# Second layer's first product by Strassen's scheme, and another series for small h

## The chip, the cores and the metric

The kernel runs on one core of one Trainium2 chip. The metric is the device time of one execution in microseconds (us), as the median of several runs. TensorE is called PE here and its weight loads PEld, VectorE DVE, ScalarE ACT, and SP is the engine that issues all the DMAs. fc counts the 16 blocks of 128 hidden columns of a layer.

## The reference, cut to what matters

```python
p_packed = sm_attn(p, k, v)             # 8 batches, 8 heads, 576 tokens, 64 wide, 32 packed
out = sm_attn(q, p_packed, p_packed)    # softmax attention twice
x = out as (4608 tokens, 512)
# first layer
h = x @ moe_w_in                        # 512 -> 2048
x = (h * tanh(softplus(h))) @ moe_w_out # 2048 -> 512
# second layer
h = x @ moe2_w_in                       # 512 -> 2048
return (h - tanh(h)) @ moe2_w_out       # 2048 -> 512
```

All is fp32. The difference h - tanh(h) loses digits for small h; there the kernel takes a series in h*h instead, chosen element by element.

## The kernel before

A product in fp32 accuracy is done as three passes of fp32r matmuls (PASSES): each operand is a high half and a low half (high times high, high times low, low times high). For each fp32 tile, ACT copies the high half and DVE subtracts to get the low half.

The kernel has two stages. The first (attention and first layer) works through 8 batches of two halves of 288 tokens: attention makes x, `layer1` takes h of two fc at a time (L580), applies Mish on ACT (L584), splits (L586, L587) and accumulates the second product (L598). Its outputs y go to DRAM (`y_d`). During this stage the weights of the second layer, which arrive as 64-bit words, are also decoded (`dec_unit`), split (`dec_split`) and written to DRAM as `w2i_d` and `w2o_d`.

The second stage works through 9 blocks of 512 tokens, and in each through 16 fc (`layer2`, 144 in all). Of one fc, PE makes h[128, 512] in one PSUM bank from four K blocks of 128 with three passes each: 12 matmuls of 512 columns (L665). ACT and DVE turn h into g: Square of h (L671), two more Squares with a pointer bias (L672, L673), Tanh (L674), three products on DVE for the series (L675, L677, L679), the difference (L681), the comparison (L683), the choice (L685), the high half (L686) and the low half (L687). PE then makes the second product: for four output blocks oc three matmuls of 512 columns each (L696), accumulated over all 16 fc in four banks `acc`. Four more banks (`bk`) hold the h's in flight. All weights of the second layer lie in SBUF in this stage: w2i in the tiles `m`, `x` and `xw`, w2o in `wo`. `load_y` brings a block's y, four K blocks, and splits each (L647, L648).

The order of the work is set by a planner, `Plan`. Each operation has an engine, a duration, a key (its due time) and the buffers that it takes and gives back; the planner steps through its own time and gives each free engine the ready operation with the smallest key. Buffers of a kind that has a queue are handed out in the order of keys. The instructions are emitted in that order, so each engine's order is fixed at build time, and semaphores keep the dependencies.

## Time and profile before

| | |
|---|---|
| median of three runs | 1557.94 us (1557.05 to 1559.39) |
| the profiled execution | 1557.33 us, its span 1555.6 us |
| mean granted clock of PE | 0.992 |
| PE busy | 1517.1 us, 98% |
| DVE busy | 1018.8 us, 65% |
| ACT busy | 899.0 us, 58% |

The span is the time from the first to the last instruction in the trace; an execution's time is a little longer. Busy times of PE are modelled ends of pipelined matmuls, so neighbours overlap, and the rate is read from starts, not from durations. An idle time in brackets stands with what ended it.

### The profile page before, as it was taken

Reading aid. Unit: us, or ns where it says so; the run is one execution under the profiler, and the core shown is the slowest. Engines: PE = TensorE matmul, PEld = TensorE weight load, DVE = VectorE, ACT = ScalarE, POOL = GpSimd, SP = SyncE. Lnnn points to the kernel's source line nnn. Section 1 sums busy time; section 2 is a strip of 40 time slices with the busy share of each in tenths; the row PEclk is TensorE's granted clock in tenths of the full one; section 3 lists DMA queues with packets and bytes.
Section 4 is the critical chain, followed back from the end, with each engine's and each line's share of the span. In section 5 each row is a group of like instructions: output and inputs, shape, how many; then the busy total and the mean of one; then the engine's idle time right before and its main releaser. Section 6 shows DMA issues by size and latency. Waiting matters only on the chain.

```text
span 1555.6 us, 24595 instructions
## 1 busy us (share of the span) xinstructions
PE 1517.1 (98%) x9816; PEld 1305.9 (84%) x9816; DVE 1018.8 (65%) x1699; ACT 899.0 (58%) x1640; POOL 0.2 (0%) x4
## 2 busy tenths in 40 slices
PE   4699999999999999999999999999999999999998
PEld 1498889999998989899988888888888888888887
DVE  6956665555634333332198888888888888888886
ACT  5866766656554545554365556565655555565654
POOL 0000000000000000000000000000000000000000
PEclk9699999999999999999999999999999999999999
DMA  8677664755625232244801001010100001010000
GB/s 296 204 269 268 224 225 171 232 191 179 215 84 163 71 118 88 82 140 143 292 1 28 28 11 44 1 55 1 54 2 27 28 15 41 1 55 1 28 1 27
DMA packets 78275, 159.48 MB, mean 103 GB/s; under 512 B 7888, under 2 KB 25424, under 8 KB 78160
## 3 DMA queue, kind: packets, MB, share of 16 engines
q1 hardware_dynamic: 78160, 157.91, 30.5%
q8 instruction: 77, 1.26, 0.3%
q14 instruction: 38, 0.31, 0.1%
HBM read 118.03 MB, written 39.85 MB: 101 GB/s over the span
## 4 chain that ended last, share of the span: by engine, by line
PE 93%; DVE 3%; ACT 2%; DMA 1%; issue 0%; SPq 0%; DVEq 0%; ACTq 0%
PE acc L598 26%; PE acc L696 25%; PE bk L665 25%; PE bk L580 13%; PE bk L548 2%; PE bk L418 1%; DMA st<-in_w1o 1%; PE bk L466 1%; PE bk L492 0%; PE bk L445 0%; DMA x<-in_k 0%; ACT st L311 0%; DMA st<-in_w1i 0%; DVE m L556 0%; DVE rr L318 0%
## 5 line engine op out<-in xcount | busy, mean ns | idle before, releaser
L696 PE MATMUL acc<-g,wo 128*128 128x512 f32 x1728 | 482.0, 389 | 0.6 <-ACT g L686 0.3
L598 PE MATMUL acc<-g,wo 128*128 128x288 f32 x3072 | 440.3, 297 | 0.0
L598 PEld LDWEIGHTS acc<-g,wo 128*128 128x128 f32 x3072 | 417.6, 189 | 17.1 <-issue 15.8
L696 PEld LDWEIGHTS acc<-g,wo 128*128 128x128 f32 x1728 | 324.3, 188 | 68.6 <-ACT g L686 0.8
L671 ACT ACTIVATE e<-bk 128x512 f32<-128x512 f32 x144 | 86.1, 598 | 316.2 <-PE bk L665 315.3
L587 DVE TENSOR_TENSOR g<-e,g 128x576 fp32r<-128x576 f32 x128 | 96.9, 757 | 229.8 <-ACT g L586 228.5
L580 PEld LDWEIGHTS bk<-a,m 128*128 128x128 f32 x1536 | 212.9, 190 | 31.1 <-issue 10.1
L580 PE MATMUL bk<-a,m 128*128 128x288 f32 x1536 | 232.0, 300 | 5.4 <-ACT a L518 4.3
L584 ACT ACTIVATE e<-bk 128x288 f32<-128x288 f32 x256 | 103.6, 412 | 154.9 <-PE bk L580 150.5
L681 DVE TENSOR_TENSOR tt<-bk,tt 128x512 f32<-128x512 f32 x144 | 99.5, 691 | 122.5 <-ACT tt L674 122.5
L665 PE MATMUL bk<-a,m 128*128 128x512 f32 x432 | 121.3, 390 | 0.8 <-DVE s L679 0.8
L665 PE MATMUL bk<-yh,m 128*128 128x512 f32 x432 | 121.2, 389 | 0.0
L685 DVE COPY_PREDICATED s<-mk,tt 128x512 f32<-128x512 uint32 x144 | 108.7, 755 | 4.4
L677 DVE SCALAR_TENSOR_TENSOR s<-s,s 128x512 f32<-128x512 f32 x144 | 99.5, 691 | 13.6 <-DVE s L675 0.9
L672 ACT ACTIVATE s<-e,c_qb 128x512 f32<-128x512 f32 x144 | 104.2, 723 | 1.1 <-DVE g L687 1.1
L673 ACT ACTIVATE s<-e,c_qd 128x512 f32<-128x512 f32 x144 | 103.7, 720 | 0.3 <-DVE s L677 0.2
L679 DVE SCALAR_TENSOR_TENSOR s<-s,bk 128x512 f32<-128x512 f32 x144 | 98.9, 687 | 4.5
L687 DVE TENSOR_TENSOR g<-s,g 128x512 fp32r<-128x512 f32 x144 | 98.3, 683 | 3.8 <-ACT g L686 3.8
L675 DVE SCALAR_TENSOR_TENSOR s<-s,e 128x512 f32<-128x512 f32 x144 | 98.7, 686 | 0.2 <-ACT s L672 0.2
L686 ACT ACTIVATE g<-s 128x512 fp32r<-128x512 f32 x144 | 90.9, 631 | 9.1 <-DVE s L685 9.1
L665 PEld LDWEIGHTS bk<-a,m 128*128 128x128 f32 x432 | 80.8, 188 | 18.1 <-DVE s L679 1.6
L665 PEld LDWEIGHTS bk<-yh,m 128*128 128x128 f32 x432 | 81.0, 188 | 16.7
...
## 6 DMA issues: line engine op xcount, KB each, us to landing
...
```

Of the source, the lines that this page charges most:

```text
L580: T.matmul(h.tile[:, :HALF], r(m.tile[:, fc % 4, kc, wl, :]), r(x.tile[:, kc, al, :]), start=(i == 0), stop=(i == 5))
L584: fr.append(op("ACT", a_cost(HALF, True), lambda c=c, h=h: A.activation(e.tile[:, c, :], h.tile[:, :HALF], AF.Mish), kf + 1, [g1] + fr, [e ...
L598: T.matmul(ac.tile[:, :HALF], r(wo[fc].tile[:, wl, oc * 128:(oc + 1) * 128]), r(gt.tile[:, gl, c, :]), start=(fc == 0 and i == 0), stop=(f ...
L665: T.matmul(h.tile, r(wv[:, wl, :]), r(yh[blk, kc].tile[:, yl, :]), start=(kc == 0 and i == 0), stop=(kc == 3 and i == 2))
L672: p1 = op("ACT", a_cost(TB, False, True), lambda: A.activation(s1.tile, zz.tile, AF.Square, bias=c_qb), k0 + 1.1, [sq], [s1])
L673: p2 = op("ACT", a_cost(TB, False, True), lambda: A.activation(s2.tile, zz.tile, AF.Square, bias=c_qd), k0 + 1.2, [sq], [s2])
L675: q = op("DVE", v_cost(TB), lambda: V.scalar_tensor_tensor(out=s1.tile, in0=s1.tile, scalar=Q_C, in1=zz.tile, op0=ALU.add, op1=ALU.mult), ...
L677: q = op("DVE", v_cost(TB), lambda: V.scalar_tensor_tensor(out=s1.tile, in0=s2.tile, scalar=Q_E, in1=s1.tile, op0=ALU.add, op1=ALU.mult), ...
L679: q = op("DVE", v_cost(TB), lambda: V.scalar_tensor_tensor(out=s1.tile, in0=s1.tile, scalar=Q_A, in1=h.tile, op0=ALU.mult, op1=ALU.mult), ...
L681: d = op("DVE", v_cost(TB), lambda: V.tensor_tensor(out=tt.tile, in0=h.tile, in1=tt.tile, op=ALU.subtract), k0 + 1.6, [th], give=[h])
L685: q = op("DVE", v_cost(TB), lambda: V.copy_predicated(s1.tile, mk.tile, tt.tile), k0 + 1.8, [q, d, k], give=[mk, tt])
L696: T.matmul(ac.tile, r(w2c[fc].tile[:, wl, oc * 128:(oc + 1) * 128]), r(gt.tile[:, gl, :]), start=(fc == 0 and i == 0), stop=(fc == NFC - 1 ...
```

## The change

Two fc that lie 8 apart (p and p+8, `NPAIR` = 8 pairs) and two halves of 256 tokens of a block make a 2 by 2 block product, with the two halves of K (256 each) summed over. Before it was 8 products of 128 x 256 x 256, now it is 7, in Winograd's form of Strassen's scheme. With A the weights (first index the fc half, second the K half) and B the tokens (first index the K half, second the token half):

```
S1 = A10 + A11   S2 = S1 - A00   S3 = A00 - A10   S4 = A01 - S2
T1 = B01 - B00   T2 = B11 - T1   T3 = B11 - B01   T4 = T2 - B10
P1 = A00 B00   P2 = A01 B10   P5 = S1 T1   P6 = S2 T2   P3 = S4 B11   P7 = S3 T3   P4 = -A11 T4
h00 = P1 + P2   h01 = P1 + P6 + P5 + P3   h11 = P1 + P6 + P7 + P5   h10 = P1 + P6 + P7 + P4
```

Every product is 2 K blocks x 3 passes = 6 matmuls of 256 columns (`product`, L761). P1, P6, P7 and P4 accumulate in one bank, and ACT copies the bank out in between (`c1`, `cy`, and `c21` at the end); P5 and P3 share a second bank (`c5` after P5), P2 has a third. DVE adds bank and copy into the tile of h in SBUF (`c11`, `c12`, `c22`, L775). So h is read from SBUF afterwards, not from PSUM.

The sums S and their splits are made in the first stage (`dec_pair`): from two decoded tiles seven tiles of high and low halves, each written to `w2i_d` (256 KB). In the second stage a pair's weights are loaded anew for every block (1,024 and 768 KB into `m`, four buffers), and are not kept. `load_y` makes the sums T and seven splits for each block, with two loads of 512 KB.

The series for small h is now (sigmoid(Q_L z + Q_B) + Q_E) * tanh(Q_T z) * Q_A * h with z = h*h: two activations as before, both of the table set `sigmoid_and_others`, which also holds Square, Tanh and Copy, so that the stage still has one table load; and two products on DVE for three. The comparison is written over z (the tile `e`). The border between series and difference moves from z = 0.3 to 0.2. The planner's period of a pair, TP, is 10.5 (5.25 an fc before), and due times are given in fifteenths of it.

```diff
-NB = NBLK * NFC
+NB = NBLK * NFC // 2
 SCALE = 1.0 / math.sqrt(D)
-ZSEL = 0.3
+ZSEL = 0.2
 LOW = 0.937 * 2.0 ** -29
-Q_B, Q_C, Q_D, Q_E = 0.6608551084240504, 6.240764296453553, -2.29454690082585, 2.410061604415441
-Q_A = 0.006504088563070549
+
+Q_T, Q_L, Q_B, Q_A, Q_E = 0.4706837657198442, -1.185665545740827, -5.582744233256905, 63.98041875880057, 0.007320721938160889
...
-    for nm, n in (("tt", 2), ("yf", 2), ("s1", 2), ("s2", 2), ("mk", 2), ("yh", 3), ("o", 1)):
+    for nm, n in (("yh", 7), ("tt", 2), ("pc", 6)):
...
-    w2i_d = dr.tile([16, 128, 2, 2, 2, 128], F32, name="w2i_d")
+    w2i_d = dr.tile([NPAIR, 128, 7, 2, 2, 128], F32, name="w2i_d")
...
+    def dec_pair(p, key):
+
+
+        u = Buf(K["so"], [128, 2, 512])
+        f = []
+        for i in range(2):
+            f.append(dec_unit(w2i[p + 8 * i], key + 0.5 * w2_step * i,
+                              lambda i=i: u.tile[:, i, :].rearrange("p (k f) -> p k f", k=4), [u] if i == 0 else [],
+                              False, True, f))
+
+        def q(i, j):
+            return u.tile[:, i, 256 * j:256 * j + 256]
+
+
+        steps = ((0, None, (0, 0), 1), (1, None, (0, 1), 1), (6, None, (1, 1), -1),
+                 (5, "s3", None, 1), (2, ((1, 0), ALU.add, (1, 1)), (1, 0), 1),
+                 (3, ((0, 0), ALU.subtract, (1, 0)), (0, 0), 1), (4, ((0, 1), ALU.subtract, (0, 0)), (0, 1), 1))
+        last, ends = f, []
...
+            h = op("ACT", a_cost(256), lambda ov=ov, sv=sv, sign=sign: A.activation(
+                r(ov(0)), sv(), AF.Copy, scale=float(sign)), k, last, take)
+            l = op("DVE", v_cost(256), lambda ov=ov, sv=sv, sign=sign: V.scalar_tensor_tensor(
+                out=r(ov(1)), in0=sv(), scalar=float(sign), in1=ov(0), op0=ALU.mult, op1=ALU.subtract),
+                k, [h] + last, give=[u])
+            last = [l]
+            w2_st[p, slot] = dma(lambda p=p, slot=slot: w2i_d[p, :, slot].rearrange("p k l f -> p (k l f)"),
+                                 lambda o=o: o.tile.rearrange("p k l f -> p (k l f)"), 256, k + 1, [l], give=[o])
...
-            w2b[fc] = Buf(K["x" if fc < 10 else "xw"], [128, 2, 2, 128])
-            w2b_rd[fc] = dma(lambda fc=fc: w2b[fc].tile, lambda fc=fc: w2i_d[fc, :, 1], 256,
-                             ka(NA - 12), [w2_st[fc], sw], [w2b[fc]])
...
+        def split(j, kd, i, t, after, k):
+            o = Buf(K[kd], [128, 2, 2, HB])
+            h = op("ACT", a_cost(TB), lambda: A.activation(r(o.tile[:, :, 0, :]), b(i, t), AF.Copy), k, after, [o])
+            l = op("DVE", v_cost(TB), lambda: V.tensor_tensor(
+                out=r(o.tile[:, :, 1, :]), in0=b(i, t), in1=o.tile[:, :, 0, :], op=ALU.subtract), k + 0.5, [h],
+                give=[f[i]])
+            yq[blk, j], yq_rd[blk, j] = o, l
+            return l
+
+        s11 = split(0, "a2", 0, 0, ld[:1], k0)
+        s21 = split(1, "a2", 1, 0, ld[1:], k0 + 1.3)
+        t1 = sub(0, 0, (0, 1), (0, 0), [s11], k0 + 2.0)
+        st1 = split(2, "yh", 0, 0, [t1], k0 + 2.6)
+        t3 = sub(0, 1, (1, 1), (0, 1), [t1] + ld, k0 + 3.3)
+        s22 = split(4, "yh", 1, 1, ld[1:], k0 + 3.9)
+        t2 = sub(1, 1, (1, 1), (0, 0), [s22, t1, t3], k0 + 4.6)
+        st2 = split(3, "yh", 1, 1, [t2], k0 + 5.2)
+        t4 = sub(1, 0, (1, 1), (1, 0), [t2, s21], k0 + 6.0)
+        split(5, "yh", 0, 1, [t3], k0 + 6.5)
+        split(6, "yh", 1, 0, [t4], k0 + 7.8)
...
+        wm, wm_rd = [], []
+        for i, (j0, j1) in enumerate(((0, 4), (4, 7))):
+            wm.append(Buf(K["m"], [128, j1 - j0, 2, 2, 128]))
+            wm_rd.append(dma(lambda i=i: wm[i].tile, lambda j0=j0, j1=j1: w2i_d[p, :, j0:j1], 256 * (j1 - j0),
+                             k0 - 26 + 6 * i, [w2_st[p, j] for j in range(j0, j1)] + [sw], [wm[i]]))
+
+        def product(j, slot, bk, deps, take, first):
+            w = (wm[j // 4], wm_rd[j // 4])
+
+            def f():
+                wv = wm[j // 4].tile[:, j % 4]
+                i = 0
+                for kc in range(2):
+                    for wl, yl in PASSES:
+                        T.matmul(bk.tile[:, :HB], r(wv[:, kc, wl, :]), r(yq[blk, j].tile[:, kc, yl, :]),
+                                 start=(first and i == 0), stop=(i == 5),
+                                 skip_group_check=not first)
+                        i += 1
+            return op("PE", 0.72, f, ks(slot), [w[1], yq_rd[blk, j]] + deps, take, [w[0], yq[blk, j]])
...
+        ba, bb, bc = (bank(K["cap_2"]) for _ in range(3))
+        hb = [Buf(K["x"], [128, TB]) for _ in range(2)]
+        c1, c5, cy = (Buf(K["pc"], [128, HB]) for _ in range(3))
+
+        def copy(c, bk, slot, deps):
+            return op("ACT", a_cost(HB, True), lambda: A.activation(c.tile, bk.tile[:, :HB], AF.Copy), ks(slot), deps, [c])
+
+        def add(half, tok, bk, c, slot, deps, take, give):
+            return op("DVE", v_cost(HB), lambda: V.tensor_tensor(
+                out=hb[half].tile[:, HB * tok:HB * tok + HB], in0=bk.tile[:, :HB], in1=c.tile, op=ALU.add),
+                ks(slot), deps, take, give)
+
+        p1 = product(0, 0, ba, [act2[0]], [ba], True)
+        s1 = copy(c1, ba, 1, [p1])
+        p2 = product(1, 1, bb, [], [bb], True)
+        c11 = add(0, 0, bb, c1, 2, [p2, s1], [hb[0]], [bb, c1])
+        p5 = product(2, 2, bc, [], [bc], True)
+        s5 = copy(c5, bc, 3, [p5])
+        p6 = product(3, 5, ba, [p1, s1], [], False)
+        sy = copy(cy, ba, 6, [p6])
+        p3 = product(4, 6, bc, [p5, s5], [], False)
+        c12 = add(0, 1, bc, cy, 7, [p3, sy, c11], [], [bc, cy])
+        p7 = product(5, 9, ba, [p6, sy], [], False)
+        c22 = add(1, 1, ba, c5, 10, [p7, s5], [hb[1]], [c5])
+        p4 = product(6, 12, ba, [p7, c22], [], False)
+        c21 = op("ACT", a_cost(HB, True), lambda: A.activation(hb[1].tile[:, :HB], ba.tile[:, :HB], AF.Copy),
+                 ks(13), [p4, c22], give=[ba])
+        second(blk, p, hb[0], [c11, c12], ks(8), k0 + 2 * TP, (3, 4, 7, 8))
+        second(blk, p + 8, hb[1], [c21, c22], ks(14), k0 + 2 * TP, (10, 11, 13, 14))
...
-        sq = op("ACT", a_cost(TB, True), lambda: A.activation(zz.tile, h.tile, AF.Square), k0 + 1, [z, act2[0]], [zz], [h])
-        p1 = op("ACT", a_cost(TB, False, True), lambda: A.activation(s1.tile, zz.tile, AF.Square, bias=c_qb), k0 + 1.1, [sq], [s1])
-        p2 = op("ACT", a_cost(TB, False, True), lambda: A.activation(s2.tile, zz.tile, AF.Square, bias=c_qd), k0 + 1.2, [sq], [s2])
-        th = op("ACT", a_cost(TB, True), lambda: A.activation(tt.tile, h.tile, AF.Tanh), k0 + 1.3, [z, act2[0]], [tt], [h])
+        sq = op("ACT", a_cost(TB), lambda: A.activation(zz.tile, h.tile, AF.Square), k0, rd, [zz])
+        p1 = op("ACT", a_cost(TB, False, True), lambda: A.activation(
+            s1.tile, zz.tile, AF.Sigmoid, bias=c_qb, scale=Q_L), k0 + 0.1, [sq], [s1])
+        p2 = op("ACT", a_cost(TB), lambda: A.activation(s2.tile, zz.tile, AF.Tanh, scale=Q_T), k0 + 0.15, [sq], [s2])
+        th = op("ACT", a_cost(TB), lambda: A.activation(tt.tile, h.tile, AF.Tanh), k0 + 0.2, rd, [tt])
         q = op("DVE", v_cost(TB), lambda: V.scalar_tensor_tensor(
-            out=s1.tile, in0=s1.tile, scalar=Q_C, in1=zz.tile, op0=ALU.add, op1=ALU.mult), k0 + 1.3, [p1])
+            out=s1.tile, in0=s1.tile, scalar=Q_E, in1=s2.tile, op0=ALU.add, op1=ALU.mult), k0 + 1.0, [p1, p2], give=[s2])
+        k = op("DVE", v_cost(TB, True), lambda: V.tensor_scalar(
+            out=zz.tile.bitcast(U32), in0=zz.tile, scalar1=ZSEL, scalar2=None, op0=ALU.is_gt), k0 + 1.1, [p1, p2])
         q = op("DVE", v_cost(TB), lambda: V.scalar_tensor_tensor(
-            out=s1.tile, in0=s2.tile, scalar=Q_E, in1=s1.tile, op0=ALU.add, op1=ALU.mult), k0 + 1.4, [q, p2], give=[s2])
-        q = op("DVE", v_cost(TB), lambda: V.scalar_tensor_tensor(
-            out=s1.tile, in0=s1.tile, scalar=Q_A, in1=h.tile, op0=ALU.mult, op1=ALU.mult), k0 + 1.5, [q], give=[h])
+            out=s1.tile, in0=s1.tile, scalar=Q_A, in1=h.tile, op0=ALU.mult, op1=ALU.mult), k0 + 1.2, [q], give=[h])
         d = op("DVE", v_cost(TB), lambda: V.tensor_tensor(
-            out=tt.tile, in0=h.tile, in1=tt.tile, op=ALU.subtract), k0 + 1.6, [th], give=[h])
-        k = op("DVE", v_cost(TB, True), lambda: V.tensor_scalar(
-            out=mk.tile, in0=zz.tile, scalar1=ZSEL, scalar2=None, op0=ALU.is_gt), k0 + 1.7, [sq, q], [mk], [zz])
-        q = op("DVE", v_cost(TB), lambda: V.copy_predicated(s1.tile, mk.tile, tt.tile), k0 + 1.8, [q, d, k], give=[mk, tt])
+            out=tt.tile, in0=h.tile, in1=tt.tile, op=ALU.subtract), k0 + 1.3, [th], give=[h])
+        q = op("DVE", v_cost(TB), lambda: V.copy_predicated(s1.tile, zz.tile.bitcast(U32), tt.tile), k0 + 1.4, [q, d, k],
+               give=[zz, tt])
         a = op("ACT", a_cost(TB), lambda: A.activation(r(gt.tile[:, 0, :]), s1.tile, AF.Copy), k0 + 2, [q], [gt])
```

PE, in the middle of the second stage. Before, first products (L665, bank `bk`) and second products (L696, of an earlier fc) alternate in threes:

```order
L665 MATMUL bk_10997<-yh_10916,x_8038 128x512 x3
L696 MATMUL acc_0_10413<-g_10963,wo_8860 128x512 x3
L665 MATMUL bk_11043<-a_1_10246,m_8456 128x512 x3
L696 MATMUL acc_0_10379<-g_11016,wo_8880 128x512 x3
L665 MATMUL bk_11043<-yh_10252,m_8456 128x512 x3
L696 MATMUL acc_0_10392<-g_11016,wo_8880 128x512 x3
L665 MATMUL bk_11043<-a_2_10904,x_8045 128x512 x3
L696 MATMUL acc_0_10402<-g_11016,wo_8880 128x512 x3
```

Now a pair takes 15 rows: here P6 and P3, two second products (L827), P7, three second products, P4, one more, and P1 and P2 of the next pair:

```order
L761 MATMUL bk_11396<-yh_10872,m_11224 128x256 x6
L761 MATMUL bk_11415<-yh_10817,m_11268 128x256 x6
L827 MATMUL acc_0_11200<-g_11310,wo_8771 128x512 x3
L827 MATMUL acc_0_11227<-g_11310,wo_8771 128x512 x3
L761 MATMUL bk_11396<-yh_10881,m_11268 128x256 x6
L827 MATMUL acc_0_11181<-g_11359,wo_8795 128x512 x3
L827 MATMUL acc_0_11189<-g_11359,wo_8795 128x512 x3
L827 MATMUL acc_0_11200<-g_11359,wo_8795 128x512 x3
L761 MATMUL bk_11396<-yh_10891,m_11268 128x256 x6
L827 MATMUL acc_0_11227<-g_11359,wo_8795 128x512 x3
L761 MATMUL bk_11513<-a_2_10035,m_11340 128x256 x6
L761 MATMUL bk_11522<-a_0_10808,m_11340 128x256 x6
```

What moved: a product of one K half is six narrow matmuls in a row, and the bank `bk_11396` is met four times within a pair, with an ACT copy or a DVE add due between two visits.

DVE at the same place. Before, one fc is seven rows without any other:

```order
L687 TENSOR_TENSOR g_12084<-s_1_12047,g_12084 128x512
L675 SCALAR_TENSOR_TENSOR s_0_12090<-s_0_12090,e_12076 128x512
L677 SCALAR_TENSOR_TENSOR s_0_12090<-s_0_12096,s_0_12090 128x512
L679 SCALAR_TENSOR_TENSOR s_0_12090<-s_0_12090,bk_12037 128x512
L683 TENSOR_SCALAR mk_12113<-e_12076 128x512
L685 COPY_PREDICATED s_0_12090<-mk_12113,tt_12078 128x512
L681 TENSOR_TENSOR tt_12121<-bk_12080,tt_12121 128x512
```

Now from the sum c12 of a pair to its last series product; the rows L812 to L817 of two fc alternate with the sums L775:

```order
L775 TENSOR_TENSOR x_11452<-bk_11415,pc_11454 128x256
L812 TENSOR_TENSOR tt_11468<-x_11452,tt_11468 128x512
L817 TENSOR_TENSOR g_11476<-xw_11412,g_11476 128x512
L775 TENSOR_TENSOR x_11490<-bk_11396,pc_11433 128x256
L806 SCALAR_TENSOR_TENSOR xw_11482<-xw_11482,xw_11488 128x512
L808 TENSOR_SCALAR e_11466<-e_11466 128x512
L810 SCALAR_TENSOR_TENSOR xw_11482<-xw_11482,x_11452 128x512
L814 COPY_PREDICATED xw_11482<-e_11466,tt_11468 128x512
L812 TENSOR_TENSOR tt_11520<-x_11490,tt_11520 128x512
L817 TENSOR_TENSOR g_11529<-xw_11482,g_11529 128x512
L806 SCALAR_TENSOR_TENSOR xw_11532<-xw_11532,xw_11542 128x512
L808 TENSOR_SCALAR e_11511<-e_11511 128x512
```

What moved: the three series products are two, and c12 and c22 stand between the rows of the two fc, so that PE's P4 waits behind the low half (L817) of an older fc.

DVE at a block's end (pair 23 of 72). Before, each K block's low half (L648) stood alone between the rows of an fc. Now, from the choice (L814) of the pair before on, with splits (L720) and differences (L714) of the next block's y:

```order
L814 COPY_PREDICATED xw_11766<-e_11745,tt_11754 128x512
L720 TENSOR_TENSOR a_2_11789<-yh_10893,a_2_11789 128x2x256
L775 TENSOR_TENSOR x_11801<-bk_11768,pc_11809 128x256
L720 TENSOR_TENSOR yh_11798<-yh_10893,yh_11798 128x2x256
L714 TENSOR_TENSOR yh_10893<-yh_10893,yv_10934 128x2x256
L817 TENSOR_TENSOR g_11831<-xw_11766,g_11831 128x512
L775 TENSOR_TENSOR x_11845<-bk_11747,pc_11784 128x256
L714 TENSOR_TENSOR yh_10893<-yh_10893 128x2x256
L806 SCALAR_TENSOR_TENSOR xw_11837<-xw_11837,xw_11843 128x512
L808 TENSOR_SCALAR e_11823<-e_11823 128x512
L810 SCALAR_TENSOR_TENSOR xw_11837<-xw_11837,x_11801 128x512
L812 TENSOR_TENSOR tt_11851<-x_11801,tt_11851 128x512
```

What moved: seven rows of y stand within one and a half pairs here (four more are spread over three pairs earlier in the block), and c12 and c22, rows L775, stand behind them.

## Rows read from the trace of the kernel before

**Rows 1.** The page's busy time, share of the span and instructions of each engine

```profile
PE 1517.1 (98%) x9816; PEld 1305.9 (84%) x9816; DVE 1018.8 (65%) x1699; ACT 899.0 (58%) x1640; POOL 0.2 (0%) x4
```

**Rows 2.** Stretches: length; PE, PEld, DVE, ACT, POOL busy (instructions); clock, DMA share, GB/s

```profile
200.00:740.00 540.00, 540.00 (x4807) 496.76 (x4796) 243.90 (x421) 307.01 (x578) 0.00 (x0) 1.00 0.46 151
740.00:760.00 20.00, 20.00 (x151) 19.87 (x150) 3.64 (x5) 6.45 (x13) 0.00 (x0) 1.00 0.90 326
800.00:1540.00 740.00, 740.00 (x3266) 612.75 (x3265) 608.99 (x984) 418.53 (x743) 0.00 (x0) 1.00 0.07 22
```

**Rows 3.** Timeline of ACT, second layer: start, us, what [idle before, its end]

```profile
1003.31 0.60 ACT L671 ACTIVATE e<-bk 128x512 f32<-128x512 f32 x1 [2.61 <-PE bk L665]
1003.81 0.59 ACT L674 ACTIVATE tt<-bk 128x512 f32<-128x512 f32 x1
1004.28 0.63 ACT L686 ACTIVATE g<-s 128x512 fp32r<-128x512 f32 x1
1004.80 0.72 ACT L672 ACTIVATE s<-e,c_qb 128x512 f32<-128x512 f32 x1
1005.42 0.72 ACT L673 ACTIVATE s<-e,c_qd 128x512 f32<-128x512 f32 x1
```

**Rows 4.** Timeline of DVE, second layer, the same stretch

```profile
1000.20 0.69 DVE L675 SCALAR_TENSOR_TENSOR s<-s,e 128x512 f32<-128x512 f32 x1
1000.99 0.69 DVE L677 SCALAR_TENSOR_TENSOR s<-s,s 128x512 f32<-128x512 f32 x1
1001.72 0.69 DVE L679 SCALAR_TENSOR_TENSOR s<-s,bk 128x512 f32<-128x512 f32 x1
1002.32 0.42 DVE L683 TENSOR_SCALAR mk<-e 128x512 uint32<-128x512 f32 x1
1002.77 0.75 DVE L685 COPY_PREDICATED s<-mk,tt 128x512 f32<-128x512 uint32 x1
1004.43 0.69 DVE L681 TENSOR_TENSOR tt<-bk,tt 128x512 f32<-128x512 f32 x1 [0.91 <-ACT tt L674]
```

**Rows 5.** Timeline of PE, first layer, then second

```profile
246.18 3.34 PE L598 MATMUL acc<-g,wo 128*128 128x288 f32 x24
249.36 1.75 PE L580 MATMUL bk<-a,m 128*128 128x288 f32 x12
250.95 3.34 PE L598 MATMUL acc<-g,wo 128*128 128x288 f32 x24
...
1002.43 0.84 PE L665 MATMUL bk<-yh,xw 128*128 128x512 f32 x3
1003.11 0.84 PE L696 MATMUL acc<-g,wo 128*128 128x512 f32 x3
```

**Rows 6.** Timeline of PE, narrow matmuls in the first layer's stretch

```profile
125.80 0.60 PE L445 MATMUL bk<-ident,a 128*128 128x128 f32 x4
126.24 0.27 PE L447 MATMUL bk<-ident,a 128*64 128x128 f32 x1
```

**Rows 7.** The page's groups with other widths: busy us and mean ns of one

```profile
L587 DVE TENSOR_TENSOR g<-e,g 128x576 fp32r<-128x576 f32 x128 | 96.9, 757 | 229.8 <-ACT g L586 228.5
...
L584 ACT ACTIVATE e<-bk 128x288 f32<-128x288 f32 x256 | 103.6, 412 | 154.9 <-PE bk L580 150.5
```

**Rows 8.** Timelines of DVE and of ACT at the end, a value handed over

```profile
1546.77 0.75 DVE L685 COPY_PREDICATED s<-mk,tt 128x512 f32<-128x512 uint32 x1
...
1547.62 0.63 ACT L686 ACTIVATE g<-s 128x512 fp32r<-128x512 f32 x1 [2.92 <-DVE s L685]
```

**Rows 9.** Timelines of PE and of ACT where the layers meet

```profile
769.19 2.16 PE L598 MATMUL acc<-g,wo 128*128 128x288 f32 x15
...
781.42 2.89 PE L696 MATMUL acc<-g,wo 128*128 128x512 f32 x12
...
773.11 0.60 ACT L671 ACTIVATE e<-bk 128x512 f32<-128x512 f32 x1
```

**Rows 10.** Timeline of PE, its last matmuls

```profile
1549.03 2.79 PE L696 MATMUL acc<-g,wo 128*128 128x512 f32 x11 [0.23 <-DVE g L687]
```

134 lines of the change are left out of this document (77 added, 57 removed).

## Prediction

> **What bounds the kernel now.** I read the page's busy line first: PE is busy 98% of the span, DVE 65%, ACT 58% [rows 1]. The share is an average over two layers, so I then read three stretches [rows 2]. From 200 to 740 (first layer) and from 800 to 1540 (second layer) PE is busy the whole stretch at full granted clock; in the second one DVE is busy 609.0 of 740 us (82%), ACT 418.5 (57%), and DMA 7%. The timelines of the second layer show who waits: ACT waits 2.61 us for a product of PE [rows 3], DVE waits 0.91 us for ACT [rows 4], PE waits for nobody. So PE's matmul rate is the limit, and the change is worth what it takes off PE, as long as DVE and ACT still keep up.
>
> **The price of a matmul.** Three 512-column matmuls start 0.68 us apart [rows 5], 226.7 ns each; 36 matmuls of 288 columns take 250.95 - 246.18 = 4.77 us [rows 5], 132.5 ns each. A straight line through the two has 0.42 ns a column and gives 119 ns at 256 columns, a width that no row has. Bounds from the nearest rows: four 128-column matmuls, each with a 128x128 load, and the one behind them start 0.44/4 = 110 ns apart [rows 6], and 256 columns will not beat that; 132.5 ns is the upper end. I take 119, because both wide rows are of the same kind and the line through them fits a rate and a fixed part.
>
> The Trainium skill (TensorE: Matmul & The Clock Gate, LDWEIGHTS) gives a weight load as columns over 1.2, which is 106.7 ns for 128, as long as the stream of 256 columns itself; a rule that speaks against narrow products, since nothing would be left to hide the load in. The same page (Back-to-back issue gap) gives 109 ns at 256 columns and 215.7 at 512; by those two the saving below would be an estimated 43 us. The rows at 512 are 11 ns slower than the page, so the rows decide.
>
> **PE.** Before, two fc of a block (fc and fc+8, now a pair) take 48 matmuls of 512: 48 x 226.7 ns = 10.88 us. Now the pair takes 24 of 512 (second product, unchanged) and 7 x 6 = 42 of 256: 5.44 + 42 x 0.119 = 5.44 + 5.00 = 10.44 us. Saved: 0.44 us a pair, 72 pairs, **31.8 us**. At 110 ns the saving would be 59 us, at 132.5 ns a loss of 9 us. An eighth of one product's columns go (1,536 a pair, 0.65 us), and the fixed part of 18 more matmuls a pair gives a third of that back.
>
> **DVE, per pair.** One instruction occupies the engine for its row less the 0.09 us by which neighbours overlap (0.69 against a start 0.60 later, 1001.72 to 1002.32) [rows 4]; one that needs the result ahead of it starts 0.73 later (1000.99 to 1001.72). Removed: one SCALAR_TENSOR_TENSOR per fc (three become two). Per fc there stay two of 0.60, the comparison 0.33, the copy 0.66 + 0.13 for its wait on the row ahead, the difference and the low half 0.60 each: 3.52, twice 7.04. Added: three adds of 256 columns. From 576 columns at 757 ns [rows 7] and 512 at 690, a column costs 1.05 ns, so 0.42 busy, 0.33 in a row: 1.0 us. Preparing y of a block now takes 7 splits and 4 differences, 11 x 0.60 = 6.6 us (4 x 0.60 before), 0.83 a pair. Sum 8.9 of 10.44 us, 85%.
>
> **ACT, per pair.** Square, two Tanh and the high half, 0.52 each, Sigmoid with a pointer bias 0.62 (as L672) [rows 3]: 2.70, twice 5.40. Four copies of 256 columns out of PSUM, by 412 ns at 288 [rows 7] and 600 at 512: 0.385 busy, 0.29 in a row, 1.15. Seven splits of y a block: 0.46 a pair. Sum 7.0 of 10.44, 67%. No row shows Sigmoid; the bounds are 0.52 (no bias) and a doubled 1.2, and I take L672's.
>
> **Does the chain keep up?** Load is not enough; the products of a pair depend on copies and adds in turn, so I walked one pair in the new order of PE and DVE shown with the change, with handovers of 0.03 us ACT to DVE (1004.40 to 1004.43) [rows 3, 4], 0.04 PE to ACT (1003.27 to 1003.31) [rows 3, 5], 0.10 DVE to ACT [rows 8]. With P1 starting at 0, PE starts P6 at 3.50, P3 at 4.22, P7 at 6.29, P4 at 9.04, the next P1 at 10.44. P3's sum c12 runs at 5.1 to 5.6, Square and Tanh of the first half at 5.7 and 6.2, high half of an older fc at 6.7, its low half on DVE at 7.4, then c22 at 8.1 to 8.5. P4 needs c22 and stands at 9.04: **0.4 us to spare** with the small lag that builds up. The next P6 needs the copy c1, which ACT ends at 13.5; it stands at 13.94, again 0.4 to spare. If PE were infinitely fast the same round through DVE and ACT would take 10.2 us, against PE's 10.44. So in the steady state PE stays the bound, by a thin margin.
>
> At a block's end (the last order shown) seven y operations sit among DVE's rows within one and a half pairs. Walked likewise, the adds fall 1.6 us behind, P6 of the next pair slips 0.1 us, P4 of the pair after it 0.3, and two pairs later the lag is gone: 0.4 us a block, 8 block ends, **+3.3 us**. Bounds: 0, and 2 us each (+16), if the lag of 1.6 us reached PE in full.
>
> **Transfers.** The weights of the products are no longer resident: 1,792 KB a pair, two loads on SP. At 10.44 us that is 172 GB/s against 22 now; 326 GB/s takes 90% of the DMA engines [rows 2], so about half of them. A load is issued when the pair two before has freed its buffer, more than a pair ahead of its use. Behind it on SP stand only output stores and the next y. I cost it at nothing; if the cover were gone PE would wait for weights, 72 times.
>
> **First layer.** Eight pairs of weight tiles are combined and split there: per pair 7 x 0.33 + 4 x 0.33 - 2 x 0.60 = 2.4 us more DVE, 20 us in all, and about 9 us more ACT, in some 270 us in which DVE is half idle (243.9 busy of 540) [rows 2]. PE's order is the old one but for some 130 rows early on, where batch 1's scores come a few microseconds later. Cost +1 us, bounds 0 and +6; a gain is excluded because PE has no idle there to lose.
>
> **Where the layers meet.** Before, the last first-layer matmuls end at 769.19 + 15 x 0.1325 = 771.2 [rows 9] with eight triples of the second layer among them (8 x 0.68 = 5.4 us); alone they would end at 765.7. From there 144 x 5.44 = 783.4 gives 1549.1, and the last matmul ends at 1551.7 [rows 10], so start and end lose 2.6 us. Now no product stands ahead of the first layer's last row, and P6 waits for c1, which follows the table load (L671 began 1.9 us after PE's last row) [rows 9]: idle 0.2 us there and about 0.5 us more until the first second product at about 777 (781.42 before) [rows 9]. I keep 2.6. At the end 13 triples are left when P4 is issued, 8.8 us, and the last chain takes some 8: covered.
>
> **Sum**, against the profiled execution: 765.7 + 72 x 10.44 = 1517.4; + 2.6 + 3.3 = 1523.3; tail 1555.6 - 1551.7 = 3.9, so 1527.2; first layer + 1 = 1528.2 span; that execution's time lies 1.7 above its span: 1529.9. The median of the runs lies 0.6 above it: **1530.5 us**.
>
> **Rivals.** *The round through DVE and ACT becomes the bound.* For it: 0.2 us of margin a pair against some ten handovers, and waits on two engines that may cost more than the 0.03 of a single one (L675 to L677, which waits also for ACT, takes 0.79, not 0.73) [rows 4]. Against: DVE would still idle 15%. At 0.04 us more a handover the round is 10.6, with y of the next block partly uncovered 10.65: 72 x 0.21 = +15, **1546**.
> *The weight load sets the rate of narrow matmuls*, place: the 42 rows of a product. For it: both kinds of rows fit, since no row shows how much of the 132.5 ns the load needs, and PEld is busy 497 of 540 us [rows 2]. Against: 110 ns with a load each [rows 6], though those are plain fp32. Price 42 x 13.5 ns = 0.57 us a pair; from 129.5 ns (5.44/42) the change loses. At 132.5: 72 x 0.57 = +41, **1571**, slower than before.
> *The first layer is hit*, attention waiting behind the combined weights: + 6 to + 12 us, **1540**.
>
> **How the numbers follow.** Forecast 0.65 (1524 to 1537), DVE round 0.17 (1538 to 1560; a fifth of it at or above today's time), first layer 0.08, weight load 0.10. Of these, 0.86 is faster by over 0.2% (about what a measurement of this kernel can tell from no change; under 1554.8), 0.04 within, 0.10 slower. The range 1523 to 1555 leaves out the weight load and the tails.
>
> **What would show it.** Six 256-column matmuls starting 0.71 us apart say the line is right, 0.79 says the load is the floor. PE 100% busy from 800 to the end with 10.44 us a pair is the forecast; idle of PE ahead of P4 or P6, released by DVE's c22 or ACT's c1, is the DVE round. Idle of PE released by a load of m, or before 740, would make me wrong in ways I priced at nothing or little.

## The result, and the profile after

The changed kernel takes **1535.8 us** (median of 4 runs, 1535.1 to 1539.1), the kernel before 1557.5 beside it: a ratio of 0.986, interval 0.985 to 0.988. That is 22 us less; 1530.5 was forecast, with a range from 1523 to 1555. Run again beside the later experiments it took 1535.4. The profiled execution was the slowest of its four (1539.1 us, span 1536.9); where its excess of 3 us plays a part, a second trace of the same kernel (1535.45 us, span 1533.3) stands beside it and is called the second trace.

The page's busy line of the changed kernel, against [rows 1]:

```profile
PE 1494.9 (97%) x11112; PEld 1342.6 (87%) x11112; DVE 1039.5 (68%) x1905; ACT 1007.6 (66%) x1995; POOL 0.2 (0%) x4
```

The stretches of the same trace, with the columns of [rows 2] (length; PE, PEld, DVE, ACT, POOL busy; clock, DMA share, GB/s):

```profile
200.00:740.00 540.00, 540.00 (x4818) 496.49 (x4817) 262.73 (x486) 316.17 (x613) 0.00 (x0) 1.00 0.47 158
740.00:760.00 20.00, 20.00 (x153) 20.00 (x153) 10.34 (x16) 9.79 (x19) 0.00 (x0) 1.00 0.97 352
760.00:800.00 40.00, 37.11 (x255) 35.12 (x254) 24.14 (x46) 24.77 (x51) 0.00 (x0) 0.96 0.79 279
800.00:1520.00 720.00, 720.00 (x4494) 647.24 (x4493) 610.20 (x1112) 513.74 (x1043) 0.00 (x0) 1.00 0.58 193
```

PE is busy all of the second layer at full granted clock, as before. DVE is at 610.2 of 720 us (85%), ACT at 513.7 (71%), and the loads of the products' weights bring the transfers from 22 to 193 GB/s. Of these stretches PE loses time only in the one where the layers meet (760 to 800).

PE's timeline of one pair of the second layer, from its first product (the row of 1046.46) to the next (1057.01), is the place to read the pair's price:

```profile
1046.46 1.59 PE L761 MATMUL bk<-a,m 128*128 128x256 f32 x12
1047.89 0.88 PE L761 MATMUL bk<-yh,m 128*128 128x256 f32 x6
1048.61 1.55 PE L827 MATMUL acc<-g,wo 128*128 128x512 f32 x6
1050.00 1.59 PE L761 MATMUL bk<-yh,m 128*128 128x256 f32 x12
1051.43 1.55 PE L827 MATMUL acc<-g,wo 128*128 128x512 f32 x6
1052.82 0.88 PE L761 MATMUL bk<-yh,m 128*128 128x256 f32 x6
1053.53 2.23 PE L827 MATMUL acc<-g,wo 128*128 128x512 f32 x9
1055.60 0.88 PE L761 MATMUL bk<-yh,m 128*128 128x256 f32 x6
1056.31 0.86 PE L827 MATMUL acc<-g,wo 128*128 128x512 f32 x3
1057.01 1.59 PE L761 MATMUL bk<-a,m 128*128 128x256 f32 x12
```

From start to start the 42 narrow matmuls take 1.43 + 0.72 + 1.43 + 0.71 + 0.71 = 5.00 us, 119 ns each, exactly what the line through [rows 5] gave. The 24 wide ones, which the change doesn't touch, take 1.39 + 1.39 + 2.07 + 0.70 = 5.55 us, not the 5.44 of 226.7 ns each [rows 5]. A pair is 10.55 us, 0.11 more than forecast, and PE waits for nobody in it.

Where the layers meet, PE's timeline of the profiled execution (the value in brackets is the idle time ahead of a row and who ended it):

```profile
773.86 1.64 PE L761 MATMUL bk<-yh,m 128*128 128x256 f32 x12
778.33 2.26 PE L761 MATMUL bk<-a,m 128*128 128x256 f32 x12 [2.83 <-DMA m<-w2i_d]
780.38 2.57 PE L761 MATMUL bk<-yh,m 128*128 128x256 f32 x12
782.79 1.55 PE L827 MATMUL acc<-g,wo 128*128 128x512 f32 x6
```

PE waits 2.83 us for the third pair's weights, and then runs at the lower of its two clocks for a while (0.50, which is 1.2 GHz, from 779.3 to 782.5; 0.96 over the stretch): 12 matmuls take 780.38 - 778.33 = 2.05 us where they otherwise take 1.43. In the second trace the wait is 1.72 us and the clock stays at 1.00. It is the one wait of PE after the first layer that either trace shows.

The last matmuls, against [rows 10]: one run of 51 that ends at 1521.76 + 11.60 = 1533.36, 3.5 us ahead of the span's end, with no idle time in it.

```profile
1521.76 11.60 PE acc L827 x51
```

### The profile page after: what moved, and what is told of

Its sections match the earlier page's. It is cut to its first block, busy times and chain, and to the rows that moved or that the text cites. A ratio compares the mean times of both kernels' runs of the same rounds, so it can differ in the third digit from the quotient of the medians.

```text
span 1536.9 us, 28140 instructions
## 1 busy us (share of the span) xinstructions
PE 1494.9 (97%) x11112; PEld 1342.6 (87%) x11112; DVE 1039.5 (68%) x1905; ACT 1007.6 (66%) x1995; POOL 0.2 (0%) x4
## 3 DMA queue, kind: packets, MB, share of 16 engines
q8 instruction: 87, 1.43, 0.4%
## 4 chain that ended last, share of the span: by engine, by line
PE 95%; DMA 2%; DVE 1%; ACT 1%; SPq 0%; issue 0%; DVEq 0%
PE acc L659 27%; PE acc L827 26%; PE bk L761 23%; PE bk L641 13%; PE bk L609 2%; PE bk L479 1%; PE bk L527 1%; PE bk L553 1%; DMA x<-in_v 1%; DMA m<-w2i_d 1%; DMA st<-in_w1o 0%; PE bk L506 0%; DMA x<-in_q 0%; DMA x<-in_k 0%; ACT st L311 0%
## 5 line engine op out<-in xcount | busy, mean ns | idle before, releaser
L827 PE MATMUL acc<-g,wo 128*128 128x512 f32 x1728 | 444.2, 393 | 0.0
L827 PEld LDWEIGHTS acc<-g,wo 128*128 128x128 f32 x1728 | 306.7, 189 | 50.1
L761 PEld LDWEIGHTS bk<-yh,m 128*128 128x128 f32 x2160 | 291.9, 191 | 20.7 <-DVE x L775 2.7
L761 PE MATMUL bk<-yh,m 128*128 128x256 f32 x2160 | 306.2, 284 | 0.1
L648 DVE TENSOR_TENSOR g<-e,g 128x576 fp32r<-128x576 f32 x128 | 96.7, 755 | 220.2 <-ACT g L647 214.0
L812 DVE TENSOR_TENSOR tt<-x,tt 128x512 f32<-128x512 f32 x144 | 99.3, 690 | 69.6 <-ACT tt L805 69.5
L801 ACT ACTIVATE e<-x 128x512 f32<-128x512 f32 x144 | 90.7, 630 | 70.6 <-DVE x L775 69.2
L761 PEld LDWEIGHTS bk<-a,m 128*128 128x128 f32 x864 | 113.3, 191 | 8.9 <-DMA m<-w2i_d 3.0
L761 PE MATMUL bk<-a,m 128*128 128x256 f32 x864 | 115.5, 283 | 2.8 <-DMA m<-w2i_d 2.8
L806 DVE SCALAR_TENSOR_TENSOR xw<-xw,xw 128x512 f32<-128x512 f32 x144 | 99.4, 690 | 26.0 <-ACT xw L804 24.3
L814 DVE COPY_PREDICATED xw<-e,tt 128x512 f32<-128x512 uint32 x144 | 109.6, 761 | 1.6
L775 DVE TENSOR_TENSOR x<-bk,pc 128x256 f32<-128x256 f32 x216 | 89.9, 417 | 23.3 <-PE bk L761 23.0
L817 DVE TENSOR_TENSOR g<-xw,g 128x512 fp32r<-128x512 f32 x144 | 98.8, 686 | 6.9 <-ACT g L816 6.8
L802 ACT ACTIVATE xw<-e,c_qb 128x512 f32<-128x512 f32 x144 | 102.2, 710 | 0.0
L810 DVE SCALAR_TENSOR_TENSOR xw<-xw,x 128x512 f32<-128x512 f32 x144 | 98.6, 685 | 0.0
```

Source lines behind the costliest of these rows:

```text
L648: lo = op("DVE", v_cost(576), lambda: V.tensor_tensor(out=r(gt.tile[:, 1]), in0=e.tile, in1=gt.tile[:, 0], op=ALU.subtract), kf + 1.2, [hi ...
L761: T.matmul(bk.tile[:, :HB], r(wv[:, kc, wl, :]), r(yq[blk, j].tile[:, kc, yl, :]), start=(first and i == 0), stop=(i == 5), skip_group_che ...
L802: p1 = op("ACT", a_cost(TB, False, True), lambda: A.activation(s1.tile, zz.tile, AF.Sigmoid, bias=c_qb, scale=Q_L), k0 + 0.1, [sq], [s1])
L806: q = op("DVE", v_cost(TB), lambda: V.scalar_tensor_tensor(out=s1.tile, in0=s1.tile, scalar=Q_E, in1=s2.tile, op0=ALU.add, op1=ALU.mult), ...
L810: q = op("DVE", v_cost(TB), lambda: V.scalar_tensor_tensor(out=s1.tile, in0=s1.tile, scalar=Q_A, in1=h.tile, op0=ALU.mult, op1=ALU.mult), ...
L812: d = op("DVE", v_cost(TB), lambda: V.tensor_tensor(out=tt.tile, in0=h.tile, in1=tt.tile, op=ALU.subtract), k0 + 1.3, [th], give=[h])
```

## The experiments

The theory at the start: PE is the bound throughout; the 0.11 us a pair are paid on PE where narrow and wide matmuls alternate; the loss where the layers meet is a load that stands too late on SP. Rivals: contention with 200 GB/s of transfers, DMA that is full whatever the order, and DVE's rows as a bound. Times are medians. The runs were made in three groups, each with the kernel before beside it (1558.7, 1558.1 and 1557.7 us). The diffs show the lines that matter; three dots stand for others.

**Weights loaded for the first two pairs alone.**

```diff
...
-        wm, wm_rd = [], []
-        for i, (j0, j1) in enumerate(((0, 4), (4, 7))):
+        wm, wm_rd = kept[n % 2] if n > 1 else ([], [])
+        kept[n % 2] = (wm, wm_rd)
+        for i, (j0, j1) in enumerate(((0, 4), (4, 7)) if n < 2 else ()):
...
```

> Weights of the seven products are loaded for the first two pairs alone and used again by all 72 (so the sums of all other pairs are made with the wrong weights); the 200 GB/s of the second layer fall to about 22. Theory (the 0.11 us that a pair takes above 10.44 is paid on PE, where narrow and wide matmuls meet): a pair stays at 10.55 us, only the wait where the layers meet goes, about 1531 us. Rival (the 0.11 us are contention from the transfers): a pair falls to 10.44 us, 72 x 0.11 = 8 us more, about 1523 us.

1531.7 us, ratio 0.983 (0.982 to 0.985). Its stretch of the second layer:

```profile
800.00:1520.00 720.00, 720.00 (x4492) 648.60 (x4491) 609.80 (x1113) 514.21 (x1042) 0.00 (x0) 1.00 0.07 23
```

Two starts of a pair on PE's timeline:

```profile
1008.74 1.59 PE L763 MATMUL bk<-a,m 128*128 128x256 f32 x12
...
1019.31 1.60 PE L763 MATMUL bk<-a,m 128*128 128x256 f32 x12
```

At 23 GB/s a pair still takes 10.55 to 10.57 us: contention with the transfers is out as the cause of the 0.11 us. The first second product starts 11.5 us after the first layer's last row instead of 13.2 (second trace), which is the wait for m. Another effect was not foreseen: one pair of each block, its second, takes 10.76 us in the changed kernel and 10.56 here. The planner, free of the loads, puts the y operations elsewhere in DVE's order.

**wo of pairs 2 to 7 loaded one pair at a time.** The expectation puts them behind the product weights of their own pair; by the edit it is those of the pair before. Either way the six loads right ahead of the third pair's m are gone.

```diff
...
+        if n < 8:
+            load_wo(n, sw, first_loads[-1:] if n > 1 else [])
+            first_loads.append(wm_rd[1])
```

> The second product's weights of pairs 2 to 7 are loaded one pair at a time behind the product weights of their own pair, instead of all ahead of them. Theory (PE's 2.83 us idle at 778 and the lower clock behind it come from the load of m for the third pair, which stood behind six loads of wo on SP): that idle time is gone, the first second product starts near 778 instead of 782.8, time about 1531 us, 4 to 5 us less than the changed kernel. Rival (DMA is full in that stretch whatever the order, so another load is late instead): no change, 1535 to 1536 us.

In the second trace of the changed kernel SP issues the six loads of wo, and then the third pair's m at 769.40:

```profile
758.26 8.28 SPq L292 DMA_DIRECT2D wo<-w2o_d  x6
...
769.40 0.32 SPq L292 DMA_DIRECT2D m<-w2i_d  x1
```

With wo held back the time is 1533.2 us, ratio 0.985 (0.983 to 0.987). The wait for m is still 1.50 us (1.72 in the second trace), so this expectation failed: the six loads of wo were not all that m stood behind. The 2.2 us by which the median lies below the 1535.4 of the changed kernel are not the edit's: in this trace the first layer ends at 763.87, in the second trace at 766.03 (see the last section). SP's timeline shows what was left, the load of the next block's y ahead of the first of the three m:

```profile
767.62 0.37 SPq L292 DMA_DIRECT2D yv<-y_d  x1
768.08 4.61 SPq L292 DMA_DIRECT2D m<-w2i_d  x3
```

**The kernel before with the new series alone.**

```diff
...
-            out=s1.tile, in0=s1.tile, scalar=Q_C, in1=zz.tile, op0=ALU.add, op1=ALU.mult), k0 + 1.3, [p1])
-        q = op("DVE", v_cost(TB), lambda: V.scalar_tensor_tensor(
-            out=s1.tile, in0=s2.tile, scalar=Q_E, in1=s1.tile, op0=ALU.add, op1=ALU.mult), k0 + 1.4, [q, p2], give=[s2])
+            out=s1.tile, in0=s1.tile, scalar=Q_E, in1=s2.tile, op0=ALU.add, op1=ALU.mult), k0 + 1.3, [p1, p2], give=[s2])
...
```

> The kernel before with the new series alone (sigmoid times tanh, one DVE row per fc less), and no change to the products. Theory (PE is the bound and its work is the same): 1557 us, within 1.5 us of the kernel before, with DVE near 76% busy instead of 82% in the second layer. Rival (the series carries part of the gain): 1554 us or less.

1556.0 us, ratio 0.9986 (0.9977 to 0.9996): 2 us less, between the two expectations. DVE falls from 82% to 503.5 of 720 us (70%), and PE is as busy as before:

```profile
800.00:1520.00 720.00, 720.00 (x3178) 596.38 (x3177) 503.53 (x823) 395.58 (x724) 0.00 (x0) 1.00 0.07 23
```

What it gains is at the ends of the second layer; the first layer's last 15 matmuls start at 769.19 before and at 769.16 here. Before, PE waited three times for values that come out of the series, 0.30 us at 777.11, 0.47 at 780.62 and 0.35 at 1548.30; here none of the three waits is left. That is 1.1 us of the 2, and the spans differ by 1.4.

**The changed kernel with the old series.** It adds one DVE row a half, two a pair.

```diff
...
-            out=s1.tile, in0=s1.tile, scalar=Q_E, in1=s2.tile, op0=ALU.add, op1=ALU.mult), k0 + 1.0, [p1, p2], give=[s2])
+            out=s1.tile, in0=s1.tile, scalar=Q_C, in1=zz.tile, op0=ALU.add, op1=ALU.mult), k0 + 0.95, [p1])
+        q = q0 = op("DVE", v_cost(TB), lambda: V.scalar_tensor_tensor(
+            out=s1.tile, in0=s2.tile, scalar=Q_E, in1=s1.tile, op0=ALU.add, op1=ALU.mult), k0 + 1.0, [q, p2], give=[s2])
...
```

> The changed kernel with the old series (three DVE rows a half instead of two, two Squares on ACT) and the new products. Theory (a pair's products depend on copies and sums in turn, so the round through DVE and ACT of 10.2 us grows by two rows to about 11.5 and passes PE's 10.55): a pair takes 11 to 11.5 us, 1565 to 1605 us, with PE idle ahead of P4 or P6. Rival (only the load of DVE counts, 8.9 + 1.2 = 10.1 of 10.55 us): a pair stays at 10.55, 1536 to 1540 us.

1536.3 us, ratio 0.986 (0.985 to 0.988), the same as with the new series. The theory was wrong here and the rival right. DVE is busy 95% of the second layer, and PE loses 0.02 us:

```profile
800.00:1520.00 720.00, 719.98 (x4483) 645.13 (x4482) 680.69 (x1249) 528.73 (x1045) 0.00 (x0) 1.00 0.57 192
```

Its c22 on DVE's timeline:

```profile
1059.93 0.42 DVE L777 TENSOR_TENSOR x<-bk,pc 128x256 f32<-128x256 f32 x1 [0.75 <-PE bk L763]
```

and P4 behind it on PE's:

```profile
1061.12 0.88 PE L763 MATMUL bk<-yh,m 128*128 128x256 f32 x6
```

The planner set DVE's order anew: c22 now follows P7 with nothing queued ahead of it and ends at 1060.35, 0.77 us ahead of P4, more than in the changed kernel. The two added rows stand elsewhere, where 15% of DVE was idle. They are not quite free: from the fifth on the pairs of this trace start 10.60 us apart on average, in the second trace 10.58, some 1.3 us in all, which the medians don't tell from nothing.

**Two rows more behind each c22, DVE's order kept.** This is the counterpart: two added DVE rows a pair again, shorter ones, but put on the chain that P4 waits for.

```diff
...
+                for _ in range(more):
+                    V.tensor_tensor(out=h, in0=h, in1=h, op=ALU.max)
...
-        c22 = add(1, 1, ba, c5, 10, [p7, s5], [hb[1]], [c5])
+        c22 = add(1, 1, ba, c5, 10, [p7, s5], [hb[1]], [c5], 2)
```

> The changed kernel in its own order, with two further rows of 256 columns on DVE behind each c22 (the larger of c22 and c22, so the values stay), about 0.95 us more between P7 and P4 of each pair; DVE's load goes to 9.9 of 10.55 us. c22 now ends 0.44 to 0.63 us ahead of P4. Theory (the order is fixed, the chain P3, c12, Square, Tanh, difference, low half, c22, P4 has only that to spare): P4 comes 0.35 to 0.5 us late in each pair, PE idles there, 72 x 0.35 to 0.5 = +25 to +36 us, 1561 to 1572 us. Rival (only the sum of DVE's rows counts, as the run with the old series suggests): 1536 to 1539 us.

1562.1 us, ratio 1.003 (1.002 to 1.004): 26.7 us more than the changed kernel beside it, slower than before the change, as the theory had it. Its stretch of the second layer:

```profile
800.00:1520.00 720.00, 705.98 (x4331) 618.64 (x4330) 636.85 (x1205) 499.78 (x1009) 0.00 (x0) 1.00 0.57 190
```

One c22 and the rows added behind it, on DVE's timeline:

```profile
1060.91 0.42 DVE L777 TENSOR_TENSOR x<-bk,pc 128x256 f32<-128x256 f32 x1
1061.36 0.88 DVE L779 TENSOR_TENSOR x<-x 128x256 f32<-128x256 f32 x2
```

PE's waits in the second layer (us in all, times, longest):

```profile
PE bk L761 <- ACT pc L772: 9.9, 24, 1.0
PE bk L761 <- DVE x L777: 2.1, 7, 0.3
```

0.91 us were added (c22 would have ended at 1061.33, the last row ends at 1062.24) and 26.7/72 = 0.37 us a pair came out: 0.54 us were to spare. From starts alone, without the scatter of the medians, a pair takes 10.98 us on average from the fourth on, against 10.58 in the second trace: 0.40 more, 0.51 to spare. Here DVE is busy 636.9 us, 44 less than with the old series, and PE waits. So the margin lies in the order of the chain, not in the load. The waits shown are 12 of the 27 us. Most of them are for ACT's copies (P6, P3) and not for c22 (P4): the lag travels through ACT's queue, as the walk in the prediction allowed for.

**The kernel before with every first product cut into narrow matmuls.** No Strassen, no loads.

```diff
-                    T.matmul(h.tile, r(wv[:, wl, :]), r(yh[blk, kc].tile[:, yl, :]),
+                    for t in range(2):
+                        T.matmul(h.tile[:, 256 * t:256 * t + 256], r(wv[:, wl, :]),
+                                 r(yh[blk, kc].tile[:, yl, 256 * t:256 * t + 256]),
...
```

> The kernel before with each 512-column matmul of the first product cut into two of 256 columns (no Strassen, nothing more to load, same sums): per fc 24 narrow and 12 wide instead of 24 wide, and the wide ones stand in 553 runs of mostly three between narrow ones. Theory (narrow at 0.1195 us, wide between narrow ones at 0.2284 us and 0.018 us more for each run of them, as fitted to the changed kernel's starts): 24 x 0.1195 + 12 x 0.2284 + 3.84 x 0.018 = 5.68 us an fc against 5.44, 144 x 0.24 = +34 us, about 1592 us. Rival (the prediction's 0.119 and 0.2267 hold in any order, and the 0.11 us a pair belong to Strassen's own waits): 144 x 0.136 = +20 us, about 1577 us.

1584.2 us, ratio 1.017 (1.016 to 1.018), 26.1 us more than before and between the expectations. PE's timeline:

```profile
1044.92 0.86 PE L699 MATMUL acc<-g,wo 128*128 128x512 f32 x3
1045.62 0.87 PE L666 MATMUL bk<-a,m 128*128 128x256 f32 x6
1046.33 0.86 PE L699 MATMUL acc<-g,wo 128*128 128x512 f32 x3
```

A run of wide matmuls is a group of them between two narrow ones. Six narrow ones take 0.71 us (118.3 ns each), a run of three wide ones 0.697 (mean of the 510 such runs from 800 to 1520), 0.017 more than the 0.68 of [rows 5]. By these, 144 x (24 x 0.1183 - 12 x 0.2267) = +17.1 us for the narrow ones and 553 runs x 0.017 = 9.4 us for the alternation, 26.5 together, against 26.1 measured; without the second term 9 us would be missing. So the surcharge is there without Strassen and without transfers. The fit that gave 1592 was wrong in two terms: it took 0.1195 for a narrow one (4.1 us too much), and it charged each wide matmul more as well (0.2284 and not 0.2267, 2.9 us too much), not only each run.

**Fewer runs of wide matmuls, and the loads later,** together and then apart. P4 moves behind the four triples of its stretch, which leaves 204 runs of wide matmuls of 280; y of the next block is loaded at the fifth pair of a block and no sooner, and wo is held back as above.

```diff
...
-        p4 = product(6, 12, ba, [p7, c22], [], False)
+        p4 = product(6, 14, ba, [p7, c22], [], False)
...
-        second(blk, p + 8, hb[1], [c21, c22], ks(14), k0 + 2 * TP, (10, 11, 13, 14))
+        second(blk, p + 8, hb[1], [c21, c22], ks(15.5), k0 + 2 * TP, (10, 11, 12, 13))
...
+        if n % NPAIR == 4 and n + 4 < NB:
+            load_y(n // NPAIR + 1, sw, later_loads)
...
```

> The changed kernel with wo of pairs 2 to 7 held back, y of the next block loaded four pairs ahead and no sooner, and P4 moved behind the four triples of its stretch, so that wide matmuls stand in 204 runs instead of 280. Theory: 76 x 0.018 = 1.4 us for the fewer runs, and 3 to 4 us where the layers meet: 1530.5 to 1532.5 us. Rival (P4 so late delays the copy of its sum and the second half's series): slower than the changed kernel, over 1536 us.

> The changed kernel itself, on the chip of these runs, so that small differences can be read: within 1.5 us of 1535.8 us, with a wait of PE of about 2 to 3 us for m of the third pair.

> The run with fewer runs of wide matmuls taken apart, first half: wo of pairs 2 to 7 and y of the next block loaded later, P4 at its old place. Theory (the two halves act apart): PE waits for m of the third pair at most 0.3 us, a pair stays at 10.55 us, 1.6 us less than the changed kernel, about 1533.8 us where that one takes 1535.4. Rival (moving wo alone did nearly nothing, PE's wait there went from 1.7 to 1.5 us; y is as idle a cause): 1535 us or more.

> Second half: the loads of the changed kernel, P4 behind the four triples of its stretch. Theory (each run of wide matmuls that goes saves 0.018 us, about 76 go): a pair takes 10.53 us instead of 10.55, 72 x 0.018 = 1.3 us less, about 1534.1 us where the changed kernel takes 1535.4, and the wait for m stays near 1.7 us. Rival (the 0.018 us belong to the wide matmuls themselves and not to the change of width): a pair stays at 10.55, 1535.4 us.

Both edits: 1532.0 us, ratio 0.983 (0.982 to 0.985). The changed kernel again: 1535.4, 0.985 (0.984 to 0.987), wait for m 1.72 us, where 2 to 3 were expected. The loads alone: 1531.4, 0.984 (0.982 to 0.985). P4 alone: 1534.6, 0.985 (0.983 to 0.986). A pair of the kernel with both edits:

```profile
1048.67 1.60 PE L771 MATMUL bk<-a,m 128*128 128x256 f32 x12
...
1050.84 2.23 PE L837 MATMUL acc<-g,wo 128*128 128x512 f32 x9
...
1054.34 0.86 PE L837 MATMUL acc<-g,wo 128*128 128x512 f32 x3
...
1055.74 2.91 PE L837 MATMUL acc<-g,wo 128*128 128x512 f32 x12
...
1059.20 1.60 PE L771 MATMUL bk<-a,m 128*128 128x256 f32 x12
```

Three runs of wide matmuls where there were four, and 10.53 us: 0.02 saved a pair, with P4 alone as well (10.53). Over 72 pairs that is 1.4 us, about what one run of wide matmuls fewer a pair should give. As a time it can't be told from nothing: of P4 alone, 0.8 us came out, inside both intervals, and the wait for m was 2.39 us in its trace, where 1.7 was expected.

The place where the layers meet, in the kernel with the later loads. SP issues m a microsecond earlier than with wo alone held back (766.97 against 768.08), with no y ahead of it:

```profile
766.97 5.45 SPq L292 DMA_DIRECT2D m<-w2i_d  x3
```

and on PE's timeline the third pair's first products and the first second product:

```profile
772.04 1.70 PE L771 MATMUL bk<-a,m 128*128 128x256 f32 x12
...
775.14 1.55 PE L837 MATMUL acc<-g,wo 128*128 128x512 f32 x6
```

PE does not wait; the first second product stands 11.5 us behind the first layer's last row, as without reloads, 1.6 less than in the second trace. The load itself shows where they come from. From its issue to its landing the third pair's m takes, in the second trace and then in the kernel with both edits:

```profile
769.40 6.77 DMA m<-w2i_d
```

```profile
766.78 5.26 DMA m<-w2i_d
```

So m is issued 3.37 us after the first layer's last row in the changed kernel (769.40 after 766.03) as with later loads (766.97 after 763.60, and 766.78 after 763.41 with both edits); the first pair has to free its buffer first. But in the changed kernel its data take 1.5 us longer, behind those of the loads ahead. The expected 1.6 us are there. About 2.4 of the 4.1 us between the two medians are not the edit's: the first layer ends at 763.60 in the one trace and at 766.03 in the other, as the last section tells. With the later loads PE also waits twice for ACT in the second layer, 0.4 us in all. The medians of both versions with later loads lie below those of both kernels, but against the changed kernel only the 1.6 us are shown; which of the two versions is better these runs don't tell.

## Why the prediction was right, and where it was off

**The bound, right.** PE is 100% busy from 800 to the end in the changed kernel, and no wait for DVE's c22 or ACT's c1 shows there; only the P4 of one pair a block comes 0.1 us late, as told below. DVE's 85% is what was worked out; ACT's 71% was put at 67%.

**Narrow matmuls, right.** 119 ns were taken from a line through 288 and 512 columns; 118.3 to 119 came out, with a weight load for each (the busy line counts as many PEld as PE instructions). The weight load as a floor (132.5 ns, rival at 1571) is out. Of the Trainium skill's figures (TensorE: Matmul & The Clock Gate, Back-to-back issue gap), 109 ns at 256 columns, which the section gives for an isolated matmul, is 9 ns below what was measured in a stream with a load for each; the estimated 43 us that followed from them were twice the gain.

**Wide matmuls, mis-sized: the term that failed.** 24 x 226.7 ns = 5.44 us was taken over from a stream in which all matmuls have one width. Between narrow ones they take 5.55: 0.02 us more for a run of three and 0.03 for a run of six or nine, four runs a pair. 72 x 0.11 = +7.9 us: this alone is more than the whole miss.

**The sum against the second trace** (span 1533.3, forecast 1528.2): pairs +7.9; block ends -1.6; first layer -0.7 (its last row ends at 766.03, forecast 766.7); start and end of the second layer -0.2 (766.03 to the last matmul's end at 1529.76 is 763.7, less 72 x 10.55 = 759.6 and 1.7 for the block ends leaves 2.4; 2.6 was kept); tail -0.4 (3.5, not 3.9). Together +5.0 of the 5.1: that four terms came out lower hides 2.9 of the 7.9 us, and this was not foreseen. Two readings of the prediction were off without harm: by [rows 10] the last matmul before ends at 1551.8, not 1551.7, which only shifts 0.1 us from the tail to the start and end; and the last P4 leaves 51 matmuls, 17 triples and not 13, so the last chain is covered all the more.

**Block ends, half in size, and by other rows than thought.** P4 of one pair a block comes late, after two y differences (L714) and a low half that stand ahead of c22 (L775) on DVE. Second trace, DVE's timeline:

```profile
1027.73 0.67 DVE L714 TENSOR_TENSOR yv<-yv 128x512 f32<-128x512 f32 x1
1028.44 0.69 DVE L714 TENSOR_TENSOR yv<-yh,yv 128x512 f32<-128x512 f32 x1
1029.05 0.68 DVE L817 TENSOR_TENSOR g<-xw,g 128x512 fp32r<-128x512 f32 x1
1029.65 0.42 DVE L775 TENSOR_TENSOR x<-bk,pc 128x256 f32<-128x256 f32 x1
```

and PE's:

```profile
1030.12 0.98 PE L761 MATMUL bk<-yh,m 128*128 128x256 f32 x6
```

c22 ends at 1030.07 and P4 starts at 1030.12; in PE's order it stands behind six wide matmuls here and not nine. That pair takes 10.76 us, 0.21 more, eight times: 1.7 us where 3.3 were forecast. But it is the second pair of the next block, and its two differences are of the four rows that were counted as spread. The seven rows at the block's end, whose lag the prediction carried on to this P4, stand from 1005.75 to 1014.20; in the pair between, which starts at 1011.00, c22 ends at 1018.70, 7.70 us after the pair's start (8.51 in the pair shown further up), so their lag is gone by then. That the late P4 stands where it was expected is luck.

**Transfers at nothing, wrong at one place.** Between 800 and the end they cost nothing (the run without reloads), and the 0.57 to 0.58 of the DMA engines at 192 to 193 GB/s is what was worked out. Where the layers meet, the data of the third pair's weights came behind those of other loads, which cost 1.7 us in one trace, 2.8 and a lower clock in the other. The argument "issued when the pair two before has freed its buffer, more than a pair ahead of its use" holds when a pair lasts 10.5 us; the first pairs are products alone, some 5 us each, and DMA was 97% busy just before [740 to 760]. The prediction had costed this 72 times or not at all, and not the first time apart. That its total for the start, 2.6 us, came out at 2.4 is luck: 1.7 us of it is this wait.

**The thin margin, right as a number, too simple as a rival.** 0.4 us to spare was read off a walk through the order; the trace shows c22's end 0.63 us ahead of P4 (1054.97 against the row of 1055.60 above), and 0.51 to 0.54 came out of the run with two more rows. c22 on DVE's timeline:

```profile
1054.55 0.42 DVE L775 TENSOR_TENSOR x<-bk,pc 128x256 f32<-128x256 f32 x1
```

But a round through DVE and ACT of 10.2 against 10.44 suggested that any row more on DVE would cost time, and one row a half more, two a pair, cost some 0.02 us a pair once the order was planned with them. The rival's 1546 needed rows on this chain, not load.

**The new series** was not needed for the gain: with the old one the time is the same within what these runs can tell. It is worth 1 to 2 us in the kernel before, at the ends.
